# Early products handed to GpSimd, one first load to ScalarE, single last tiles: a dynamic-convolution kernel with a new order

## The chip, the cores and the metric

One core of a Trainium2 chip runs the whole kernel. The metric is the device time of one execution in microseconds (us); every time below is from the chip. The core has five engines with queues of their own: TensorE (PE; its weight loads are PEld), VectorE (DVE), ScalarE (ACT), GpSimd (POOL) and SyncE (SP, which here only issues transfers). Each executes its instructions in the order in which they were written, and waits at an instruction until what it depends on is done.

## The reference

```python
w = exp(weight_gen - max(weight_gen, -1));  w = w / (sum(w, -1) + 1e-9)      # [8, 4224, 8 heads, 7 taps]
out[b, s, h, :] = sum over k of w[b, s, h, k] * x_padded[b, s + k, h, :]     # causal, 6 zeros ahead; 24 columns a head
xn = (out - mean(out)) / sqrt(var(out) + 1e-6) * g_ln                        # over the 192 columns
result = out + relu(xn @ w_ch1) @ w_ch2                                      # 192 -> 768 -> 192
```

x is [8, 4224, 192] in float32; `w_ch1` and `w_ch2` arrive as float64, and the kernel rebuilds their float32 values from the words.

## The kernel before

The 33,792 tokens are cut into 128 runs of 264 consecutive tokens, one run on each partition (16 partitions for each of the 8 batches), so a "token" below is one of 264 columns of 128 tokens. Three pipelines run side by side.

*Softmax* (`softmax`), in pieces of 4, 8 and then 12 tokens: maximum on VectorE (`max`), subtraction on GpSimd (`sub`), exponential on ScalarE (`exp`), sum on VectorE (`sum`; for two pieces on TensorE), logarithm on ScalarE (`log`), and a second subtraction on GpSimd (`less`). A last exponential on ScalarE (`expw`) writes one chunk's weights to PSUM.

*Convolution* (`conv`), in chunks: two of 2 tokens, then chunks of 4, later of 6. They start at tokens 0, 2, 4, 8, 12, 16, ..., so the first is S0, the second S2, the third S4, the fourth S8, the fifth S12. A chunk has four products of x with weights: `c0` (taps 1, 2), `c1` (taps 3, 4), `c2` (tap 0) and `c3` (taps 5, 6). The three with two taps write `pr` buffers, of which there are five. VectorE makes them, but in the first `PMUL` = 3 chunks GpSimd makes `c3`, from a copy of the weights in SBUF that one more exponential (`keep`) leaves there. The first three chunks are summed over the taps by TensorE (`z0` to `z3`) and copied out by ScalarE (`copy`). From the fourth on, two transfers add pairs of products (`d0`, `d1`) and four GpSimd additions (`a0` to `a3`) finish the sum `y`.

*Norm and feed-forward* (`norm` and what follows): mean and variance of each token come from ScalarE (`sums`, `squares`, one activation with an accumulator for each token); where the part's start lies below `STATS` = 8 (the first two parts, tokens 0 to 7) from VectorE (`stats`). Then `rstd` on ScalarE, `newton` on VectorE, the scaled tokens `xh` on ScalarE. Groups of 4 tokens are split into two halves of float16 (`hi` on ScalarE, `lo` on GpSimd) and transposed by a transfer (`turn`, line 762); the first two groups are transposed by TensorE (`tp`, `thi`, `tlo`). A group has three units of first-layer products (`unit`, line 780) with two PSUM buffers to write to; each is emptied by a ScalarE ReLU (`relu`) and then a VectorE operation that writes the low half (`hlo`, line 798). After a group's second unit come the two halves of the second layer of the group before it (`p0`, `p1`, line 832), and VectorE adds the result to `y` (`f`, line 884), which is stored (`u`). The last group has no unit behind it: its four tiles are made one by one (`output`, line 853), two in one PSUM bank, and `merge` adds each pair by one VectorE operation of 384 columns and stores it.

The weights of both layers are loaded, rebuilt and split in the first 55 us (`load_weights`, `from_double`, `w_scale`, `weights`), on the same engines.

The order is written out by hand: `PLACE` gives each operation its position, by name and count, and `Plan.order` sorts by it and hands out buffers. An engine's order is the order of its operations in `PLACE`. The costs passed to `op` take no part in it here.

Of the kernel before, what the change touches and what calls it, by code (L numbers as in the profile page):

```python
# [26 lines left out]
PMUL = 3  # L27
STATS = 8
# [11 lines left out]
    'wload': (0, 1, 15, 26, 98, 102, 176, 495, 321, 482, 657, 761, 837, 1034, 613, 1145, 1282, 1182, 951, 1438,  # L40
        1515, 1614, 1730,),
    'load': (2, 3, 5, 7, 9, 22, 43, 95, 105, 145, 143, 174, 92, 244, 288, 208, 297, 414, 325, 484, 497, 660,
        569, 626, 644, 719, 851, 815, 920, 942, 918, 1001, 1066, 1240, 1236, 1303, 1205, 1365, 1353, 1467, 1476,
        1619, 1541, 1592, 1669, 1749, 1853, 1832, 1814, 1980, 2003, 1949,),
    'w_load': (45, 13, 20,),
    'w_gain': (40, 38, 29,),
    'w_load2': (32,),
    'w_as': (88,),
    'w_ap': (90,),
    'w_av': (96, 99,),  # L50
    'w_an': (107,),
    'w_cs': (53,),
    'w_cp': (52,),
    'w_cv': (58, 60,),
    'w_cn': (80,),
    'w_s1': (113, 118,),
    'w_d': (150, 124,),
    'w_h': (127, 123,),
    'w_l': (155, 126,),
    'w_lc': (166, 130,),  # L60
    'w_m': (169, 172, 135, 133,),
    'w_c2s': (73, 103, 120,),
    'w_c2p': (71, 94, 125,),
    'w_c2v': (76, 79, 108, 110, 134, 138,),
    'w_c2n': (83, 116, 142,),
    'w_s2': (148, 156, 185,),
    'w_d2': (178,),
    'w_h2': (175, 164, 183,),
    'w_l2': (184, 181, 189,),
    'w_lc2': (200, 202, 194,),  # L70
    'max': (4, 11, 54, 64, 188, 281, 355, 559, 594, 537, 769, 881, 907, 1073, 1096, 1211, 1320, 1225, 1430,
        1502, 1679, 1770, 1960,),
    'sub': (6, 16, 59, 81, 193, 378, 448, 565, 599, 679, 779, 887, 972, 1091, 1124, 1261, 1400, 1415, 1513,
        1598, 1759, 1811, 2007,),
    'exp': (8, 21, 63, 111, 215, 382, 467, 592, 637, 709, 795, 903, 1023, 1105, 1148, 1276, 1412, 1459, 1581,
        1645, 1822, 1849, 2023,),
    'sum': (10, 25, 234, 390, 492, 601, 645, 721, 834, 946, 1032, 1138, 1178, 1279, 1435, 1511, 1605, 1676,
        1835, 1860, 2034,),
    'log': (12, 28, 86, 152, 249, 409, 498, 604, 658, 765, 858, 969, 1036, 1160, 1251, 1341, 1458, 1524, 1608,
        1699, 1856, 1869, 2060,),  # L80
    'less': (14, 31, 87, 160, 276, 421, 510, 606, 691, 771, 883, 987, 1058, 1193, 1257, 1344, 1478, 1559, 1650,
        1742, 1859, 1937, 2093,),
    'expw': (17, 30, 35, 56, 97, 139, 151, 199, 235, 266, 327, 356, 329, 434, 473, 516, 540, 623, 656, 703, 722,
        783, 820, 910, 960, 996, 1017, 1080, 1111, 1210, 1203, 1280, 1359, 1372, 1402, 1503, 1494, 1594, 1564,
        1678, 1721, 1775, 1796, 1888, 1944, 1972, 2058, 2145, 2102, 2104,),
    'keep': (18, 39, 65,),
# [16 lines left out]
    'copy': (50, 69, 119,),  # L103
    'stats': (61, 74, 144, 141,),
    'rstd': (77, 147, 209, 279, 354, 426, 502, 585, 693, 802, 895, 1002, 1102, 1201, 1307, 1420, 1501, 1623,
        1713, 1817, 1926, 2018, 2119, 2214, 2280, 2338,),
    'newton': (91, 153, 219, 285, 359, 432, 507, 591, 696, 804, 901, 1003, 1106, 1204, 1309, 1433, 1510, 1627,
# [10 lines left out]
    'thi': (136, 180,),  # L118
    'tlo': (159, 186,),
# [19 lines left out]
    'sums': (131, 168, 191, 187, 222, 242, 268, 258, 323, 310, 338, 334, 380, 399, 413, 411, 478, 457, 486, 490,  # L139
# [149 lines left out]
def kernel(  # L289
# [309 lines left out]
    def norm(pa):  # L599
# [3 lines left out]
        def row(i):  # L603
            if S0 < STATS:
                i = {1: 3, 2: 4}[i]
            return at(s4)[:, i, :n]
# [538 lines left out]
```

## Time and profile before

| | before |
|---|---|
| runs (us) | 843.34, 845.62, 844.35: median 844.35 |
| profiled execution (us) | 843.82, its span 842.0, mean granted clock 0.994 |
| TensorE busy | 821.4 us, 98% of the span |
| VectorE, GpSimd, ScalarE busy | 736.5 (87%), 701.6 (83%), 683.8 us (81%) |
| first TensorE instruction, first unit, last product's end | 8.4, 52.7, 837.5 us |
| data moved | 140.88 MB, 167 GB/s over the span |

Instructions are named by the line of the kernel that made them. A row of a timeline gives the start, the time and how many like instructions were put together, and in square brackets how long the engine had stood idle before and what ended that. TensorE's granted clock is 1.00 at 2.4 GHz and 0.50 at 1.2 GHz.

### The profile page before, as it was taken

How to read it: one execution, taken by the hardware profiler on the slowest of the kernel's cores; microseconds unless marked ns; L12 is line 12 of the kernel's file. 1: busy time of each engine (PE TensorE's matmuls, PEld its weight loads, DVE VectorE, ACT ScalarE, POOL GpSimd, SP SyncE). 2: the span in 40 equal slices, each digit the busy share in tenths (PEclk: the TensorE clock that was granted, in tenths of full speed). 3: DMA queues.
4: the chain of work that ended last, by engine and by line, in shares of the span. 5: the costliest groups of instructions: out<-in, count | busy, mean ns of one | idle time of the engine just before them, and what ended most of it. 6: DMA issues, size and time to landing. Idle time of an engine off the chain costs nothing.

```text
span 842.0 us, 37407 instructions
## 1 busy us (share of the span) xinstructions
PE 821.4 (98%) x16724; PEld 811.3 (96%) x16724; DVE 736.5 (87%) x685; ACT 683.8 (81%) x1774; POOL 701.6 (83%) x402
## 2 busy tenths in 40 slices
PE   6889999999999999999999999999999999999997
PEld 5669999999999999999999999999999999999997
DVE  7999999999999999999999999999989896745332
ACT  3899998898998899898888979988888878776431
POOL 4999999999999999999999999899798879624000
PEclk9889999999999999999999999999999999999999
DMA  9997997989999997889878997777877766352432
GB/s 228 206 211 153 221 162 170 204 160 205 193 195 191 199 215 167 178 186 215 190 153 202 188 217 174 164 185 163 180 153 162 165 145 129 78 116 68 80 65 58
DMA packets 133887, 140.88 MB, mean 167 GB/s; under 512 B 104294, under 2 KB 106222, under 8 KB 133726
## 3 DMA queue, kind: packets, MB, share of 16 engines
q1 hardware_dynamic: 120190, 88.16, 45.9%
q0 software_dynamic: 13536, 50.34, 30.8%
q8 instruction: 130, 2.13, 1.0%
q14 instruction: 31, 0.25, 0.1%
HBM read 36.43 MB, written 25.95 MB: 74 GB/s over the span
## 4 chain that ended last, share of the span: by engine, by line
PE 82%; DVE 11%; issue 2%; POOL 2%; ACT 1%; DMA 1%; SPq 1%; DVEq 0%; POOLq 0%; ACTq 0%
PE po L832 41%; PE ph L780 40%; DVE pr L535 6%; DVE hlo L798 2%; DVE y L535 1%; POOL y L538 1%; DMA x<-in_x_dram 1%; PE ph L861 1%; DVE y L884 1%; POOL pr L541 1%; ACT hh L796 0%; DVE mx L466 0%; ACT junk L611 0%; DVE sm L482 0%; DVE s L628 0%
## 5 line engine op out<-in xcount | busy, mean ns | idle before, releaser
L538 POOL TENSOR_TENSOR y<-y,pr 128x1152 f32<-128x1152 f32 (+1 forms) x188 | 488.3, 2625 | 13.0 <-DVE y L535 4.3
L780 PE MATMUL ph<-xT,c_w 64*128 64x256 f16 x7128 | 412.9, 269 | 1.9 <-DVE hlo L798 1.3
L780 PEld LDWEIGHTS <-c_w 64*128 64x128 f16 x7128 | 386.2, 94 | 3.1 <-issue 2.9
L832 PE MATMUL po<-c_w2h,hh 64*128 64x192 f16 x3120 | 388.0, 243 | 1.1 <-DVE y L884 1.1
L832 PE MATMUL po<-c_w2l,hh 64*128 64x192 f16 x3120 | 388.0, 243 | 0.0
L832 PE MATMUL po<-c_w2h,hlo 64*128 64x192 f16 x3120 | 388.0, 243 | 0.0
L535 DVE TENSOR_TENSOR pr<-x,wn 128x2304 f32<-128x2304 f32 (+2 forms) x147 | 333.2, 2276 | 4.3 <-POOL y L538 2.5
L832 PEld LDWEIGHTS <-hh 64*128 64x128 f16 x6240 | 309.7, 94 | 1.4 <-issue 1.3
L798 DVE SCALAR_TENSOR_TENSOR hlo<-ph,hh 128x1024 f16<-128x1024 f32 x198 | 239.4, 1217 | 73.1 <-ACT hh L796 72.6
L796 ACT ACTIVATE hh<-ph 128x1024 f16<-128x1024 f32 x198 | 200.2, 1014 | 84.8 <-PE ph L780 80.6
L832 PEld LDWEIGHTS <-hlo 64*128 64x128 f16 x3120 | 177.6, 94 | 0.0
L758 POOL TENSOR_TENSOR hl<-xh,hl 128x768 f16<-128x768 f32 x64 | 114.7, 1828 | 49.1 <-ACT hl L756 48.3
L686 ACT ACTIVATE xh<-y,s 128x192 f32<-128x192 f32 x264 | 125.8, 536 | 17.2 <-DVE s L674 12.1
L616 ACT ACTIVATE junk<-y,s 128x192 f32<-128x192 f32 x256 | 115.8, 452 | 7.9 <-PE po L832 1.8
L541 POOL DMA_DIRECT2D pr<-pr x94 | 93.2, 1054 | 26.6 <-DVE pr L535 22.1
L611 ACT ACTIVATE junk<-y 128x192 f32<-128x192 f32 x256 | 92.1, 360 | 12.5 <-PE po L832 4.1
L884 DVE SCALAR_TENSOR_TENSOR y<-po,c_fs,y 128x768 f32<-128x768 f32 (+1 forms) x83 | 67.9, 835 | 7.4 <-PE po L832 7.2
L535 DVE TENSOR_TENSOR y<-x,wn 128x1152 f32<-128x1152 f32 (+2 forms) x50 | 59.9, 1199 | 0.0
L756 ACT ACTIVATE hl<-xh 128x768 f16<-128x768 f32 x64 | 53.4, 836 | 1.6 <-PE po L832 0.7
L611 ACT ACTIVATION_READ_ACCUMULATOR junk<-y 128x1 f32 x256 | 48.1, 188 | 0.0
L616 ACT ACTIVATION_READ_ACCUMULATOR junk<-y,s 128x1 f32 x256 | 47.9, 187 | 0.0
L486 POOL TENSOR_TENSOR e<-e,sm 128x672 f32<-128x672 f32 (+2 forms) x23 | 37.8, 1645 | 6.6 <-ACT sm L484 6.6
(86 smaller groups left out, 308.3 us busy)
## 6 DMA issues: line engine op xcount, KB each, us to landing
pr<-pr POOLq DMA_DIRECT2D x68, 576.0 KB, 6.1
x<-in_x_dram SPq DMA_DIRECT2D x34, 576.0 KB, 6.0
out_dram<-y SPq DMA_DIRECT2D x34, 576.0 KB, 4.9
pr<-pr POOLq DMA_DIRECT2D x26, 384.0 KB, 5.0
w<-in_weight_gen_dram SPq DMA_DIRECT2D x21, 336.0 KB, 5.1
x<-in_x_dram SPq DMA_DIRECT2D x14, 384.0 KB, 6.2
out_dram<-y SPq DMA_DIRECT2D x13, 384.0 KB, 5.2
x<-in_moe_w_ch_dram SPq DMA_DIRECT2D x1, 1152.0 KB, 11.3
```

The costliest lines, as they stand in the source:

```text
L535: E.tensor_tensor(out=ov, in0=xv, in1=wv, op=ALU.mult)
L538: Q.tensor_tensor(out=flat(0), in0=flat(0), in1=flat(k), op=ALU.add)
L541: return Q.dma_start(flat(to), flat(k), accum_op=ALU.add, max_dma_last_dim=CHUNK * D * 4)
L611: A.activation(junk, at(y)[:, j, :], AF.Identity, scale=-SQ / D, accum_out=at(s4)[:, 3, t : t + 1])
L616: A.activation(junk, at(y)[:, j, :], AF.Square, scale=SQ, bias=at(s4)[:, 3, t : t + 1], accum_out=at(s4)[:, 0, t : t + 1])
L686: A.activation(paired(xh, t), at(y)[:, i, :].rearrange("p (c q) -> p c q", q=P // 2), AF.Identity, bias=row(2 if quick else 3)[:, g + t : ...
L758: lambda xh=xh, hl=hl: Q.tensor_tensor(out=halves(hl, True), in0=pairs(xh), in1=halves(hl, False), op=ALU.subtract),
L780: T_.matmul(ph[:, r, v * 2 * P : (v + 1) * 2 * P], W["w1"][rows, WB[r][c], w, f : f + P], xv[rows, a, c, :, :], start=(v == 0 and k == 0), ...
L796: lambda: A.activation(at(hh)[:, us, :], at(ph), AF.Relu), [ph], [(hh, u)])
L798: lambda: V.scalar_tensor_tensor(out=at(hlo)[:, us, :], in0=at(ph), scalar=0.0, in1=at(hh)[:, us, :], op0=ALU.max, op1=ALU.subtract),
L832: made.append(T_.matmul(at(po)[:, z, e * D : (e + 1) * D], token(b, 2 * z + e, j)[rows], W[w][rows, j, :], start=(ph == 0 and e == 0 and k ...
L884: V.scalar_tensor_tensor(out=ysl, in0=at(po)[:, zs[0] : zs[-1] + 1, : 2 * D], scalar=W["fs"][:, 0:1], in1=ysl, op0=ALU.mult, op1=ALU.add)
```

## The change

Five things are edited, and `PLACE` is replaced as a whole (2400 positions before, 2408 after).

- The second of the two first loads of x is issued on ScalarE's queue. ScalarE's table load and its `minus` activation become planned operations; by the new positions they stand ahead of that load (`table` 1, `minus` 4, load 5).
- `PMUL` is 4, so GpSimd makes `c3` of the fourth chunk too; `PTWO` has it make `c1` of the second chunk.
- `STATS` is the tuple `(4,)`: the first part's statistics (tokens 0 to 3) are now ScalarE's.
- `last` replaces `output` for the last four tiles: each has a PSUM bank and a VectorE operation of 192 columns of its own. The first two are stored together, the other two one by one.
- The first exponential waits for `table`, the matmuls with `minus` for `minus`.

```diff
-PMUL = 3
-STATS = 8
+PMUL = 4
+STATS = (4,)
+PTWO = (2,)
...
-    A.preload_act_table_set("natural_log_exp_and_others")
...
-    A.activation(minus, ident, AF.Copy, scale=-1.0)
...
-            def first(o, m):
+            def first(o, m, E=SY):
                 src = bass.AP(tensor=xf.tensor, offset=(C - PAD + o) * D,
                               ap=[[C * D, PB - 1], [PB * C * D, B], [1, m * D]])
-                SY.dma_start(X[B:P, o : o + m, :].rearrange("p t d -> p (t d)"), src)
+                E.dma_start(X[B:P, o : o + m, :].rearrange("p t d -> p (t d)"), src)
...
-            sp(want, lambda: first(cut, PAD + n - cut), [], [("x", "h"), *cols], dma_ns((PAD + n - cut) * D * 4), "load")
+            op("ACT", 620, want, lambda: first(cut, PAD + n - cut, A), w=[("x", "h"), *cols],
+               dma=dma_ns((PAD + n - cut) * D * 4), kind="load")
+            op("ACT", 1300, ("table", 0), lambda: A.preload_act_table_set("natural_log_exp_and_others"), w=["table"])
+            op("ACT", 310, ("minus", 0), lambda: A.activation(minus, ident, AF.Copy, scale=-1.0), ["table"], ["minus"])
...
-            if c < PMUL and i == 3:
+            if c < PMUL and (i == 3 or i == 1 and t0 in PTWO):
                 op("Pool", q_ns(2 * nd), (f"c{i}", t0), lambda k=k: mul(k, 2, Q), [*xr, (e, "w", c)], w)
...
-        quick = S0 < STATS
+        quick = S0 in STATS
...
+    def last(gp, t, s):
+        e = t % 2
+        if e == 0:
+            gp["po"] = Buf("ph")
+        po, ks = gp["po"], triples(gp)
+
+        def mm():
+            for k, (b, j, w) in enumerate(ks):
+                T_.matmul(at(po)[:, e, :D], token(b, t, j), W[w][:, j, :], start=k == 0, stop=k == len(ks) - 1)
+
+        op("PE", 1490, ("o", s), mm, whole(gp), [(po, e), "pe"], lat=360.0)
+        y, j = ycol(gp["pa"], gp["g"] + t)
+
+        def final():
+            V.scalar_tensor_tensor(out=at(y)[:, j, :], in0=at(po)[:, e, :D], scalar=W["fs"][:, 0:1],
+                                   in1=at(y)[:, j, :], op0=ALU.mult, op1=ALU.add)
+
+        op("V", v_ns(D, 63), ("f", s), final, [(po, e), "fs"], [(y, j)])
+        if t > 0:
+            i, n = (j, 1) if t > 1 else (j - 1, 2)
+            t0 = chunks[-1]["S"] + i
+            sp(("u", s), lambda: SY.dma_start(tokens(out, t0, n), at(y)[:, i : i + n, :].rearrange("p t d -> p (t d)")),
+               [(y, i + q) for q in range(n)], [], dma_ns(n * D * 2))
...
     for t in range(NT):
-        output(prev, t, C)
+        last(prev, t, C)
```

The order that the old and the new `PLACE` give each engine at the start (operation and token at which its chunk, softmax piece or part starts; `w_...` are weight operations, and numbers count them):

```
SyncE before    w S0, w S4, x first a, x first b, x first f, x S2, x S4, w_load 1, w S12, w_load 2, x S8, w S24, gain, load2, gain, gain, x S12, w_load 0
SyncE after     w S0, x first a, w S4, x first f, x S2, w S12, x S4, w_load 1, w_load 2, x S8, load2, w_load 0, gain, gain, w S24, gain, x S12
VectorE before  max S0, sum S0, max S4, c0 S0, c2 S0, sum S4, c1 S0, c0 S2, c1 S2, c2 S2, c2 S4, c1 S4, c0 S4, max S12, w_cv 2x, stats S0, max S24, c1 S8, c0 S8, stats S2, w_c2v 2x, c2 S8, c3 S8, newton S0, w_av 2x, c2 S12, w_c2v 2x, c0 S12
VectorE after   max S0, sum S0, c0 S0, c2 S0, max S4, c1 S0, sum S4, c0 S2, c2 S2, max S12, c0 S4, c2 S4, w_cv 2x, c0 S8, c2 S8, c1 S8, w_c2v 2x, c1 S4, newton S0, w_c2v, max S24, w_av, w_c2v, w_av, c0 S12, c2 S12
GpSimd before   sub S0, less S0, sub S4, less S4, c3 S0, c3 S2, sub S12, c3 S4, d0 d1 S8, sub S24, less S12, a0 a1 a2 a3 S8, d0 a0 d1 a1 a2 S12, d0 S16, less S24, a3 S12
GpSimd after    sub S0, less S0, sub S4, c3 S0, less S4, c1 S2, c3 S2, sub S12, c3 S8, d0 a0 a1 S8, c3 S4, less S12, d1 S8, sub S24, d0 S12, a2 S8, d1 S12, a3 S8, a0 a1 a2 S12, d0 S16, a3 S12, less S24
```

TensorE's order of operations is the same in both. From about token 96 on the other engines' orders are the same again, but for the end.

## Rows read from the trace of the kernel before

**Rows 1.** Chain of waits in time order, from 800 us: start, us, what.
```profile
802.86 1.96 PE ph L780 x36
804.83 2.97 PE po L832 x72
...
831.47 6.06 PE ph L861 x72
```

**Rows 2.** Timeline of TensorE, first units: start, us, instruction, [idle before].
```profile
57.23 2.14 PE L780 MATMUL ph<-xT,c_w 64*128 64x256 f16 x36 [0.32 <-DVE hlo L798]
...
71.86 4.11 PE L780 MATMUL ph<-xT,c_w 64*128 64x256 f16 x72
```

**Rows 3.** Windows: window, length, busy PE PEld DVE ACT POOL, clock, DMA share, GB/s.
```profile
30.00:40.00 10.00, 6.95 (x34) 4.98 (x33) 9.53 (x16) 9.02 (x22) 9.37 (x7) 0.82 0.87 216
40.00:50.00 10.00, 8.26 (x32) 6.12 (x32) 9.69 (x17) 9.23 (x28) 9.92 (x8) 0.67 1.00 210
```

**Rows 4.** Timeline of VectorE, up to 31 us.
```profile
5.11 0.61 DVE L466 TENSOR_REDUCE mx<-w 128x64 f32<-128x448 f32 x1
7.30 0.95 DVE L535 TENSOR_TENSOR pr<-x,wn 128x768 f32<-128x768 f32 x1 [1.58 <-DMA x<-in_x_dram]
...
13.08 3.41 DVE L535 TENSOR_TENSOR pr<-x,wn 128x1536 f32<-128x1536 f32 x2
...
29.70 0.95 DVE L535 TENSOR_TENSOR y<-x,wn 128x768 f32<-128x768 f32 x1
```

**Rows 5.** Timeline of GpSimd, up to 40 us.
```profile
9.77 0.97 POOL L486 TENSOR_TENSOR e<-e,sm 128x448 f32<-128x448 f32 x1 [2.58 <-ACT sm L484]
...
15.44 1.55 POOL L535 TENSOR_TENSOR pr<-x,e 128x768 f32<-128x768 f32 x1 [3.20 <-PE ph L560]
...
19.91 2.90 POOL L535 TENSOR_TENSOR pr<-x,e 128x1536 f32<-128x1536 f32 x1 [1.15 <-ACT e L502]
...
25.81 2.00 POOL L486 TENSOR_TENSOR e<-e,sm 128x672 f32<-128x672 f32 x1
27.14 8.14 POOL L538 TENSOR_TENSOR y<-y,pr 128x768 f32<-128x768 f32 x4
35.22 0.87 POOL L541 DMA_DIRECT2D pr<-pr  x1
```

**Rows 6.** Instruction groups of VectorE by shape: count, busy us, mean ns, idle before.
```profile
L535 DVE TENSOR_TENSOR pr<-x,wn 128x1536 f32<-128x1536 f32 x41 | 70.9, 1744 | 0.1
...
L628 DVE BATCH_NORM_STATS2 s<-y 128x6 f32<-128x384 f32 x4 | 2.2, 560 | 0.0
...
L955 DVE SCALAR_TENSOR_TENSOR po<-pr,po 128x384 int32<-128x384 int32 x3 | 1.7, 552 | 0.0
L884 DVE SCALAR_TENSOR_TENSOR y<-ph,c_fs,y 128x384 f32<-128x384 f32 x2 | 1.2, 618 | 4.4 <-PE ph L861 4.4
```

**Rows 7.** Timeline of SyncE: transfers as they are issued.
```profile
2.11 1.93 SPq L428 DMA_DIRECT2D x<-in_x_dram  x2
...
66.05 1.54 SPq L762 DMA_TRANSPOSE xT<-hl  x1
```

**Rows 8.** Timeline of ScalarE, up to 50 us.
```profile
6.30 0.27 ACT L498 ACTIVATE wn<-e 128x112 f32<-128x112 f32 x1 [0.75 <-POOL e L486]
...
15.24 0.48 ACT L573 COPY y<-ph 128x384 f32<-128x384 f32 x1 [3.89 <-PE ph L560]
...
46.23 0.36 ACT L611 ACTIVATE junk<-y 128x192 f32<-128x192 f32 x1
...
48.23 0.60 ACT L1071 ACTIVATE c_w2h<-hlo,c_r 128x384 f16<-128x384 f32 x1
```

**Rows 9.** Transfers of the whole run by line: count, KB, median us to landing.
```profile
xT<-hl SPq DMA_TRANSPOSE x64, 3.9
```

**Rows 10.** Transfers issued after 830 us: count, KB each, median us to landing.
```profile
out_dram<-y SPq DMA_DIRECT2D x1, 384.0 KB, 3.3
out_dram<-y SPq DMA_DIRECT2D x2, 192.0 KB, 2.5
```

More of the change, by code (lines that the diff above doesn't have):

```diff
@@ L39 @@
 PLACE = {
[L40 to L85, printed above, removed]
@@ L86 @@
-    'keep': (18, 39, 65,),
[16 rows of a table removed]
[L103 to L107, printed above, removed]
[10 rows of a table removed]
-    'thi': (136, 180,),
-    'tlo': (159, 186,),
[19 rows of a table removed]
-    'sums': (131, 168, 191, 187, 222, 242, 268, 258, 323, 310, 338, 334, 380, 399, 413, 411, 478, 457, 486, 490,
[6 rows of a table removed]
@@ L146 @@
-    'squares': (154, 173, 195, 206, 259, 247, 275, 277, 332, 346, 341, 349, 388, 401, 419, 422, 481, 468, 499,
[15 rows of a table removed]
-    'turn': (239, 282, 308, 317, 400, 410, 471, 477, 549, 554, 618, 639, 652, 727, 755, 740, 825, 848, 862, 939,
[3 rows of a table removed]
-    'halo': (316, 563, 768, 1130, 1345, 1638, 2061,),
-    'unit': (197, 203, 212, 220, 227, 243, 260, 267, 284, 302, 309, 326, 344, 351, 367, 384, 391, 406, 423, 430,
[10 rows of a table removed]
-    'relu': (204, 214, 217, 231, 236, 251, 270, 283, 296, 313, 319, 340, 358, 373, 377, 393, 404, 418, 431, 442,
[10 rows of a table removed]
@@ L189 @@
-    'hlo': (207, 216, 223, 237, 253, 261, 278, 287, 305, 318, 324, 343, 362, 379, 383, 402, 412, 420, 436, 451,
[14 rows of a table removed]
-    'hop': (246, 286, 331, 368, 407, 446, 485, 522, 555, 588, 628, 665, 699, 735, 772, 809, 844, 878, 915, 948,
[16 rows of a table removed]
+    'wload': (0, 3, 10, 47, 62, 142, 182, 479, 278, 544, 664, 766, 842, 1039, 623, 1150, 1287, 1187, 956, 1443,
+        1520, 1619, 1735,),
+    'load': (2, 5, 6, 8, 13, 21, 52, 78, 88, 148, 178, 151, 245, 318, 186, 289, 339, 425, 410, 482, 627, 666,
+        565, 629, 651, 724, 856, 820, 925, 946, 923, 1006, 1072, 1245, 1240, 1308, 1210, 1369, 1358, 1472, 1481,
+        1624, 1546, 1597, 1674, 1754, 1858, 1837, 1819, 1985, 2008, 1954,),
@@ new lines @@
+    'table': (1,),
+    'minus': (4,),
+    'w_load': (28, 15, 18,),
+    'w_gain': (31, 51, 41,),
+    'w_load2': (24,),
+    'w_as': (96,),
+    'w_ap': (98,),
+    'w_av': (102, 108,),
+    'w_an': (112,),
+    'w_cs': (57,),
+    'w_cp': (58,),
+    'w_cv': (61, 66,),
+    'w_cn': (101,),
+    'w_s1': (116, 119,),
+    'w_d': (135, 124,),
+    'w_h': (154, 125,),
+    'w_l': (157, 127,),
+    'w_lc': (170, 132,),
+    'w_m': (175, 174, 140, 137,),
+    'w_c2s': (79, 91, 138,),
+    'w_c2p': (80, 92, 126,),
@@ new lines @@
+    'w_c2v': (83, 85, 97, 105, 141, 145,),
+    'w_c2n': (89, 113, 147,),
+    'w_s2': (150, 167, 204,),
+    'w_d2': (181,),
+    'w_h2': (184, 176, 180,),
+    'w_l2': (189, 185, 196,),
+    'w_lc2': (195, 190, 202,),
+    'max': (7, 25, 42, 100, 194, 230, 308, 585, 574, 625, 774, 886, 912, 1079, 1101, 1216, 1325, 1230, 1435,
+        1507, 1684, 1775, 1965,),
+    'sub': (9, 26, 56, 110, 201, 345, 426, 596, 577, 685, 784, 892, 975, 1095, 1129, 1266, 1405, 1420, 1518,
+        1603, 1764, 1816, 2012,),
@@ new lines @@
+    'exp': (11, 30, 70, 122, 217, 373, 439, 603, 643, 714, 800, 908, 1028, 1110, 1153, 1281, 1417, 1464, 1586,
+        1650, 1828, 1854, 2028,),
+    'sum': (12, 34, 259, 402, 448, 606, 648, 726, 839, 951, 1037, 1143, 1183, 1284, 1440, 1516, 1610, 1681,
+        1840, 1865, 2039,),
+    'log': (14, 37, 95, 161, 275, 422, 481, 613, 662, 770, 863, 974, 1041, 1165, 1256, 1347, 1463, 1529, 1613,
+        1704, 1861, 1874, 2065,),
+    'less': (16, 38, 103, 172, 282, 430, 484, 616, 697, 775, 887, 990, 1063, 1198, 1261, 1349, 1483, 1564, 1655,
+        1746, 1864, 1941, 2097,),
@@ new lines @@
+    'expw': (17, 32, 44, 45, 107, 149, 162, 209, 225, 251, 303, 354, 372, 446, 438, 523, 537, 631, 661, 708,
+        727, 788, 825, 916, 965, 1001, 1022, 1085, 1117, 1215, 1208, 1285, 1364, 1377, 1407, 1508, 1499, 1599,
+        1569, 1683, 1726, 1781, 1801, 1893, 1949, 1977, 2063, 2150, 2107, 2109,),
+    'keep': (19, 35, 60, 46,),
[16 rows of a table added]
+    'copy': (55, 73, 118,),
+    'sums': (63, 75, 155, 144, 192, 203, 243, 248, 257, 281, 325, 335, 348, 341, 397, 389, 409, 423, 470, 468,
[7 rows of a table added]
+    'squares': (67, 81, 166, 173, 197, 211, 260, 286, 267, 292, 327, 351, 360, 344, 416, 392, 412, 427, 475,
[7 rows of a table added]
@@ new lines @@
+    'rstd': (86, 139, 219, 294, 365, 431, 509, 592, 698, 807, 900, 1007, 1108, 1206, 1312, 1425, 1506, 1628,
+        1718, 1822, 1931, 2023, 2124, 2219, 2285, 2343,),
+    'newton': (93, 153, 223, 298, 367, 437, 514, 597, 701, 809, 906, 1008, 1111, 1209, 1314, 1438, 1515, 1632,
[10 rows of a table added]
+    'thi': (129, 187,),
+    'tlo': (146, 193,),
+    'stats': (131, 128,),
[27 rows of a table added]
+    'turn': (242, 284, 324, 334, 404, 420, 474, 464, 539, 551, 619, 646, 660, 732, 760, 745, 830, 853, 867, 943,
[3 rows of a table added]
+    'halo': (276, 614, 773, 1135, 1350, 1643, 2066,),
@@ L221 @@
+    'unit': (200, 207, 215, 224, 231, 246, 264, 270, 288, 304, 312, 329, 347, 353, 371, 386, 393, 411, 428, 434,
[10 rows of a table added]
+    'relu': (208, 216, 221, 234, 241, 255, 272, 283, 297, 315, 332, 338, 356, 366, 383, 399, 406, 421, 436, 447,
[10 rows of a table added]
+    'hlo': (210, 218, 226, 240, 256, 266, 280, 295, 301, 321, 343, 346, 363, 379, 385, 405, 414, 424, 445, 450,
[14 rows of a table added]
+    'hop': (249, 291, 331, 375, 415, 453, 487, 522, 559, 591, 633, 667, 704, 740, 777, 815, 849, 883, 920, 953,
[16 rows of a table added]
 }
@@ L468, in softmax @@
              lambda: Q.tensor_tensor(out=at(e)[:, :m], in0=a3(wb), in1=wide(mx), op=ALU.subtract), [wb, mx], [e])
-        step("ACT", a_ns(m * K), "exp", lambda: A.activation(a3(wb), at(e)[:, :m], AF.Exp), [e], [wb])
+        step("ACT", a_ns(m * K), "exp", lambda: A.activation(a3(wb), at(e)[:, :m], AF.Exp), [e, "table"], [wb])
         if S0 in PESUM:
@@ L603, in row @@
         def row(i):
-            if S0 < STATS:
+            if S0 in STATS:
                 i = {1: 3, 2: 4}[i]
@@ L1030, in mm @@
                     T_.matmul(at(z)[:, b, :h], minus, hi()[:, q], start=False, stop=True)
-            op("PE", 2.2 * n, ("w_l", 0), mm, [(dg, i), *r], [z], lat=400.0)
+            op("PE", 2.2 * n, ("w_l", 0), mm, [(dg, i), "minus", *r], [z], lat=400.0)
             op("ACT", a_ns(n, 150), ("w_lc", 0),
@@ L1076, in mm @@
                 T_.matmul(at(z)[:, h % 2, :tn], minus, w2f[:, o : o + tn], start=False, stop=True)
-            op("PE", 2.2 * tn, ("w_l2", 0), mm, [dq, (w2r, h), ("w2h", h)], [(z, h % 2)], lat=400.0)
+            op("PE", 2.2 * tn, ("w_l2", 0), mm, [dq, "minus", (w2r, h), ("w2h", h)], [(z, h % 2)], lat=400.0)
             op("ACT", a_ns(tn, 150), ("w_lc2", 0),
```

239 rows, old and new, of the table PLACE are left out of this document.

## The prediction

> **What bounds the kernel now.** I read the chain of waits first, at its late end. From 800 us on it is TensorE alone: units of first-layer products of 1.96 us (36 matmuls), halves of second-layer products of 2.97 us (72), the last four tiles in 6.06 us up to 837.53, then one VectorE operation and its store [rows 1]. Then the timeline of TensorE: the third unit starts at 57.23 us, and what it waited for is `hlo`, the VectorE operation that empties the first unit's PSUM buffer [rows 2]. From there to 837.53 are 780.3 us; the 196 units and 130 halves that are left and the last tiles are 196 x 1.96 + 130 x 2.97 + 6.06 = 776.3 us. So only 4.0 us are lost after that point. The middle is TensorE's own work, and its order of operations is the same in both kernels. What can change is the time at which that third unit starts, those 4.0 us, and the 4.5 us behind the last product (842.0 - 837.5).
>
> What sets the start is read from windows before it: between 30 and 50 us VectorE is busy 9.53 and 9.69 of 10 us, GpSimd 9.37 and 9.92, ScalarE 9.02 and 9.23, while TensorE has gaps and its granted clock has fallen [rows 3]. VectorE is full from its first product at 7.30 us on, which had waited for a load of x [rows 4]. GpSimd gets full later: before 25 us it waited 2.58, 3.20 and 1.15 us in front of three instructions [rows 5]. So I forecast by a ledger of VectorE up to the first `hlo`, and check it against GpSimd and ScalarE.
>
> **The ledger of VectorE.** Removed: an early product of the second chunk (128x768, 0.95 us), the k=5,6 product of the fourth chunk (128x1536, 1.744), two statistics (0.56 each) [rows 4, 6]. Neighbours overlap by 0.08 (two of 128x1536 take 3.41 us, 1.744 + 1.66), so net 0.87 + 1.66 + 2 x 0.48 = 3.5 us. It is worth that if nothing else comes late, and 0 if another engine sets the start.
>
> The loads: on SyncE the two first loads of x took 1.93 us of issue [rows 7], 0.97 each. ScalarE takes one; the other moves ahead of the second load of weights. The exponential that the first product needs ends at 6.57 (6.30 + 0.27 [rows 8]); the product began at 7.30. So 0.7 us at most are won, and 0 if the transfers themselves are the limit. I take 0.7, since what it waits for is issued about one weight load sooner. On ScalarE the issue stands between the table load and the softmax's first exponential, in idle time: 0, or 1.0 (SyncE's issue time) if that exponential comes late.
>
> The Trainium skill limits this: "DMA: Bandwidth & Descriptors", section "Issuing engines are not separate DMA queues", has it that loads started on several engines run on the same 16 DMA engines, and only time of issue is saved. By that rule bytes ahead of the load still count, and with a term of 0 the sum would be 0.7 smaller; no row before the change tells which.
>
> What it costs: the second load of weights comes about 1 us later, and the maximum over it (0.61 us [rows 4]) moves from idle time before 7.30 to behind two products: -0.5. The sum over it then waits for a GpSimd subtraction (0.97, the row of its shape [rows 5]) and a ScalarE exponential (0.27 at a quarter of its size [rows 8], so 0.3 to 1.1, I take 0.6), under the cover of one product (0.87): -0.7 (0 to -1.2).
>
> GpSimd: it gets a 128x768 product (1.55 us) and a 128x1536 one (2.90) [rows 5], 4.45 us together. Its new order, laid out by those rows: the subtraction of the second softmax ends at about 9.5 (two VectorE products and the maximum behind 6.6, then 0.97); the first chunk's product 11.05; the second softmax's other subtraction 12.0; two products of the second chunk 15.1; a subtraction of the third softmax (1.33, from 25.81 to 27.14) 16.4; the new 128x1536 product 19.3; a transfer issued (0.87) and two additions (2.03 each, four in 8.14) 24.3; the third chunk's product 27.2; the third softmax's other subtraction 28.5. Before, that one ended at 27.14: 3.1 of the 4.45 us go into the idle time above. By a ScalarE exponential (0.27 to 0.54, I take 0.3) it releases the first VectorE product of the fifth chunk, at 28.8. Before, VectorE came to that chunk at 29.70 [rows 4]; with the terms above (0.7 - 0.5 - 0.7 + 3.5 = 3.0) it comes at 26.7, or at 27.8 since two weight operations of 0.55 [rows 6] are put ahead of the chunk. It waits 1.0: -1.0 (0 to -3.0).
>
> A page speaks against giving products to GpSimd at all: the Trainium skill, "GPSIMD Engine Reference", section "3.1 Elementwise — side-by-side cycle accounting", has 4497 against 2293 ns for one two-input operation, a ratio of 1.96. Here it is 2.90 against 1.744, 1.66, measured in this kernel. By the page's ratio the two 128x1536 products would take 0.5 us longer each, and the gain would be 1.0 us smaller; I go by the rows.
>
> ScalarE: four sums and four squares come to it for the first four tokens. Two and two take 2.00 us (46.23 to 48.23 [rows 8]), so 4.0. It stood idle for 3.89 us at 15.24 [rows 8], about where they now stand, and for 0.98 + 0.77 between 30 and 50 [rows 3]. I cost them at 0; with no cover they delay the weight copies ahead of the first unit by 4.0, which is part of rival 2.
>
> Ledger: 3.0 - 1.0 = 2.0 us earlier at the first `hlo`, and the third unit with it; 0 and 4.2 are the ends.
>
> **Behind the start.** The transpose of the third group was issued at 66.05 [rows 7] and lands 3.9 later [rows 9], at 70.0; its unit starts at 71.86 [rows 2]. TensorE will want it 2.0 earlier with 1.9 of slack, and VectorE delivers its part about 2 us earlier. GpSimd doesn't: it is 1.4 late at 28 us, less a subtraction of 1.33 that the new order puts behind the fifth chunk's additions. I leave the 4.0 us lost there as they are (bounds: 1 saved to 2.5 added).
>
> **The end.** The last operation takes 192 columns instead of 384. A column costs (1.744 - 0.95) / 768 = 1.03 ns, so 0.2 of its 0.618 us go [rows 6]. The third tile's operation lies under the last tile's matmuls. The last store is 96 KB instead of 192: between 384 and 192 KB the landing fell from 3.3 to 2.5 us [rows 10]; 0.4 more if that goes on, 0 if what is left is fixed; I take 0.2. The matmuls are the same 72 with other banks: 0. End: 0.4 (0.2 to 0.6).
>
> **Sum.** 2.0 + 0.4 = 2.4 us. The profiled execution took 843.8 us (span 842.0); less 2.4 that is 841.4. The median of the runs, 844.35, lies 0.5 above it; less 2.4 it is 841.9, my forecast.
>
> **Rivals.**
> 1. The cover holds everywhere: 3.5 of VectorE's work in full, 0.7 of the loads, 0.4 of the end, and some 0.5 of the 4.0 lost later: 5.1, so 839.3. For it: the idle time of GpSimd in [rows 5] is 6.9 us against 4.45 added. Against: that time lies behind waits for other engines. Chance 0.20.
> 2. GpSimd or ScalarE sets the start: GpSimd is 9.92 of 10 us busy from 40 us on [rows 3], and ScalarE's 4.0 us may find only part of its idle time. The start gains 0 to 1 and the end its 0.4: 843.0 to 844.0. Chance 0.25.
> 3. Slower, by TensorE's clock. The gaps let the granted clock fall, to means of 0.82 and 0.67 in two windows [rows 3]; the lower level, 1.2 of 2.4 GHz, is 0.5, so it held for (0.18 + 0.33) x 10 / 0.5 = 10 us. It was over before the units began. With other gaps ahead of the second-layer weights the fall can come later and reach into the first units, which then lose half of that time for good: 5 us if all of it lies there. 841.9 + 5 = 846.9, or 848.9 if the start isn't earlier either. It decides at a granted clock of 0.5 under the first units; up to 2.4 us lost it only eats the gain. Chance 0.12.
>
> **How the numbers follow.** The forecast has the remaining 0.43, and a range of its own of 840.5 to 843.3. 0.3% (2.5 us) is about what a measurement can tell from no change. Faster by more is below 841.8: rival 1 and nearly half of the forecast's case (0.2), with a little of rival 2 by the spread of the runs, 0.44 in all. Slower by more is above 846.9: the upper half of rival 3 and a bad run, 0.09. The rest is 0.47. The range 839.2 to 845.2 leaves out the better half of rival 1 and most of rival 3.
>
> **What would show it.** VectorE's first product at 6.6; a wait of VectorE at 27 to 29 us for the fifth chunk's exponential; the third unit at 55.2; the last VectorE operation at 0.42 us, and 4.1 us from the last product to the end of the span. A third unit not before 57, a granted clock below 1.00 under the units, or new waits of TensorE between 65 and 110 us would prove it wrong.

## The result

The changed kernel is slower: 851.94 us (median of 6 runs, 851.65 to 852.53) against 844.39 for the kernel before (6 runs, 843.12 to 845.62). The ratio is 1.0092 with a 95% interval of 1.0079 to 1.0105, +7.5 us where 2.4 less was forecast. In the profiled executions the spans are 850.8 and 842.0 us, 8.8 apart.

**Profile after.** I read ScalarE's timeline first, since [rows 8] put the exponential ahead of the first product at 6.30. ScalarE in the changed kernel (start, length, instruction, idle before it and its releaser; ACTq is its issue of transfers), and then the first exponential in the kernel before:

```profile
0.74 1.28 ACT L437 ACT_TABLE_LOAD   x1 [0.74 <-PEq L1158]
2.33 0.31 ACT L438 ACTIVATE minus<-ident 128x128 f16<-128x128 f32 x1 [0.31 <-POOL ident L377]
7.02 1.49 ACTq L430 DMA_DIRECT2D x<-in_x_dram  x1
8.62 0.39 ACT L474 ACTIVATE w<-e 128x224 f32<-128x224 f32 x1 [5.98 <-issue]
...
10.53 0.27 ACT L503 ACTIVATE wn<-e 128x112 f32<-128x112 f32 x1 [0.75 <-POOL e L491]
```

```profile
4.38 0.39 ACT L469 ACTIVATE w<-e 128x224 f32<-128x224 f32 x1 [1.75 <-POOL e L468]
```

ScalarE is free at 2.64 and does nothing until it issues its load at 7.02. The softmax's first exponential comes behind that, at 8.62; the kernel before had it at 4.38. "<-issue" means that the profile shows nothing that ScalarE waited for. The compiled program does. In its list of ScalarE's instructions the load carries a wait:

```
2 L438 ACTIVATE minus<-ident 128x128 [waits Pool_49]
3 L430 DMA x<-in_x_dram 120x1x768 [waits DMAHW2_49]
4 L474 ACTIVATE w_64<-e_96 128x224 [waits DMAHW0_49,Pool_49]
```

DMAHW0 to DMAHW7 are eight completion counters, which the compiler gives in turn to the transfers that SyncE and ScalarE issue (GpSimd's have counters of their own). In SyncE's list of the same program the ninth and tenth transfer wait for DMAHW0 and DMAHW1, the next for DMAHW3. ScalarE's load, the fourth transfer by its place in the written order, has thus been counted as the eleventh; how the compiler comes to count it there is not shown, but with one ScalarE instruction fewer ahead of it, it is counted third (experiment 2). It gets the third transfer's counter and may not be issued before that one has landed. The third is the second softmax's weights. The chain of waits of the changed kernel shows the handover (start, length, what):

```profile
2.56 4.44 DMA w<-in_weight_gen_dram
7.02 9.44 DMA x<-in_x_dram
```

The weights land at 7.00, the load is issued at 7.02 and lands at 16.46. VectorE has both delays, in answer to [rows 4]:

```profile
9.04 0.39 DVE L487 TENSOR_REDUCE sm<-w 128x32 f32<-128x224 f32 x1 [5.36 <-ACT w L474]
10.83 0.95 DVE L540 TENSOR_TENSOR pr<-x,wn 128x768 f32<-128x768 f32 x1 [1.41 <-ACT wn L503]
...
16.48 0.95 DVE L540 TENSOR_TENSOR pr<-x,wn 128x768 f32<-128x768 f32 x1 [3.71 <-DMA x<-in_x_dram]
```

The first product is 3.5 us late (10.83 against 7.30). The product at 16.48 is the first chunk's second one of two taps (`c1` S0); it is the first to read what ScalarE's load brings, and waits 3.7 more for it. TensorE, in answer to [rows 2], and its waits from 50 to 300 us (what waited, for what: us in total, times, longest):

```profile
59.69 4.11 PE L785 MATMUL ph<-xT,c_w 64*128 64x256 f16 x72 [0.74 <-ACT c_w2l L1109]
64.20 2.14 PE L785 MATMUL ph<-xT,c_w 64*128 64x256 f16 x36 [0.41 <-DVE hlo L803]
```

```profile
PE po L837 <- issue: 1.4, 2, 1.1
PE ph L785 <- DVE hlo L803: 1.3, 3, 0.7
PE ph L785 <- DMA xT<-hl: 1.2, 1, 1.2
```

The third unit starts at 64.20 instead of 57.23: 7.0 of the 8.8 us. From there to the end of the last product (846.24) it is 782.0 instead of 780.3, 1.7 more, 1.2 of it a wait for a transposed tile that the kernel before did not have. From the last product to the end of the span it is 4.6 instead of 4.5. The granted clock fell again ahead of the units, and was back under them, where 72 matmuls take 4.11 us as in [rows 2] (window, length, busy PE PEld DVE ACT POOL, clock, DMA share, GB/s; compare [rows 3]):

```profile
40.00:50.00 10.00, 8.95 (x34) 6.23 (x33) 9.79 (x14) 8.95 (x29) 8.78 (x6) 0.73 0.84 201
50.00:60.00 10.00, 6.94 (x29) 4.47 (x29) 9.90 (x14) 7.67 (x24) 10.00 (x9) 0.76 0.86 210
60.00:70.00 10.00, 8.94 (x162) 8.53 (x159) 7.87 (x12) 9.64 (x26) 9.32 (x7) 1.00 0.76 146
```

### The profile page after: what moved, and what is told of

It is laid out like the page before. It is cut to its first block, busy times and chain, and to the rows that moved or that the text cites. A ratio compares the mean times of both kernels' runs of the same rounds, so it can differ in the third digit from the quotient of the medians.

```text
span 850.8 us, 37434 instructions
## 1 busy us (share of the span) xinstructions
PE 824.3 (97%) x16724; PEld 810.8 (95%) x16724; DVE 733.5 (86%) x683; ACT 687.7 (81%) x1791; POOL 705.7 (83%) x404
## 4 chain that ended last, share of the span: by engine, by line
PE 85%; POOL 4%; ACT 4%; DVE 3%; issue 2%; DMA 2%; SPq 0%; DVEq 0%; POOLq 0%
PE po L837 42%; PE ph L785 41%; POOL y L543 2%; DVE pr L540 2%; DMA x<-in_x_dram 1%; PE ph L565 1%; ACT junk L621 1%; DVE hlo L803 1%; POOL pr L546 1%; POOL hl L763 1%; PE ph L866 1%; ACT junk L616 1%; DMA w<-in_weight_gen_dram 1%; ACT hh L801 0%; PE ph L1104 0%
## 5 line engine op out<-in xcount | busy, mean ns | idle before, releaser
L621 ACT ACTIVATE junk<-y,s 128x192 f32<-128x192 f32 x260 | 117.6, 452 | 9.9 <-PE po L837 3.7
L491 POOL TENSOR_TENSOR e<-e,sm 128x672 f32<-128x672 f32 (+2 forms) x23 | 35.6, 1548 | 8.5 <-ACT sm L489 8.5
```

The lines of the kernel that those rows point to most:

```text
L621: A.activation(junk, at(y)[:, j, :], AF.Square, scale=SQ, bias=at(s4)[:, 3, t : t + 1], accum_out=at(s4)[:, 0, t : t + 1])
```

## Experiments

"The start" below is the start of the third unit (before 57.23, after 64.20). A time that follows "against" is that of the kernel before, run again beside the experiment; the ratio is taken to it, with its 95% interval in brackets.

**1. The load back on SyncE, all else as changed.**
```
-  op("ACT", 620, want, lambda: first(cut, PAD + n - cut, A), ...
+  op("SP", 620, want, lambda: first(cut, PAD + n - cut, SY), ...
```


> The changed kernel with one edit: the second first load of x goes back to SyncE, in the same position. Counter theory (ScalarE's load waits until the transfer of the second weights has landed, since the two are given the same completion counter, and ScalarE holds the softmax behind it): 841 to 844 us, the first exponential back at 4.4 us. Queue theory (a transfer is slow to start and to land on ScalarE's own queue): the same 841 to 844. Handover theory (GpSimd's and ScalarE's added work and the new order cost the time): stays at 850 or above.

844.62 us against 843.92, ratio 1.0006 [0.9997, 1.0016]: the whole loss is gone, and no gain is left. This kernel shows the rest of the change without the accident. VectorE:

```profile
6.58 0.95 DVE L540 TENSOR_TENSOR pr<-x,wn 128x768 f32<-128x768 f32 x1 [1.41 <-ACT wn L503]
...
29.09 1.75 DVE L540 TENSOR_TENSOR pr<-x,wn 128x1536 f32<-128x1536 f32 x1 [0.64 <-ACT wn L503]
...
52.06 1.74 DVE L540 TENSOR_TENSOR pr<-x,wn 128x1536 f32<-128x1536 f32 x1
55.11 1.22 DVE L803 SCALAR_TENSOR_TENSOR hlo<-ph,hh 128x1024 f16<-128x1024 f32 x1 [1.30 <-ACT hh L801]
```

The first product is at 6.58 (forecast 6.6), the fifth chunk at 29.09 behind a wait of 0.64 (28.8, 1.0). VectorE is free for the first `hlo` at 53.8; in the kernel before it came to that `hlo` at 55.96, without a pause. So the ledger's 2.0 us are there, as 2.2. But `hlo` waits 1.30 for ScalarE's ReLU of the first unit, and the start is 56.39, 0.84 earlier. The first unit itself starts at 51.88, behind the last weight products (TensorE; then windows as above):

```profile
47.42 0.91 PE L1104 MATMUL ph<-hlo,xh 128*128 128x384 f32 x2 [2.00 <-ACT xh L1095]
...
51.17 0.52 PE L1105 MATMUL ph<-c_w2h,minus 128*128 128x384 f16 x1
51.88 4.11 PE L785 MATMUL ph<-xT,c_w 64*128 64x256 f16 x72 [0.18 <-ACT c_w2l L1109]
```

```profile
46.00:48.00 2.00, 0.58 (x2) 0.40 (x3) 2.00 (x3) 2.00 (x6) 2.00 (x2) 1.00 0.99 243
48.00:50.00 2.00, 2.00 (x7) 0.95 (x5) 2.00 (x3) 0.57 (x1) 2.00 (x3) 0.59 0.87 265
50.00:52.00 2.00, 1.81 (x7) 0.59 (x7) 2.00 (x3) 1.84 (x7) 2.00 (x3) 0.56 1.03 270
```

The same in the kernel before:

```profile
49.18 0.91 PE L1075 MATMUL ph<-hlo,xh 128*128 128x384 f32 x2 [1.74 <-ACT xh L1066]
...
51.82 0.33 PE L1076 MATMUL ph<-c_w2h,minus 128*128 128x384 f16 x1
52.72 4.19 PE L780 MATMUL ph<-xT,c_w 64*128 64x256 f16 x72 [0.58 <-ACT c_w2l L1080]
```

```profile
48.00:50.00 2.00, 0.82 (x3) 0.46 (x4) 2.00 (x3) 2.00 (x6) 2.00 (x3) 1.00 0.95 197
50.00:52.00 2.00, 1.99 (x8) 0.78 (x6) 2.00 (x5) 1.91 (x9) 2.00 (x3) 1.00 1.02 300
```

TensorE idles for 2.00 us, from 48 us on the granted clock is 0.59 and 0.56, for the most part its lower level, and the weight products take 4.3 us (47.42 to 51.69) instead of the 3.0 (49.18 to 52.15) that they took before at 1.00. They are 1.3 us longer, as much as the start misses the ledger by; experiment 9 tests how much of it is the clock's.

**2. ScalarE's load one place sooner, ahead of the `minus` activation.**
```
-    'load': (2, 5, 6, 8, 13, ...
+    'load': (2, 3.5, 6, 8, 13, ...
```


> The changed kernel with ScalarE's load of x one place earlier, between the table load and the activation that makes minus; there it is given a counter that no transfer holds, and has no wait. Counter theory: issue at 2.0 to 3.0 us, exponential at 4.4, 841 to 844 us. Queue theory: issue late or landing over 8 us all the same, 848 us or more. Handover theory: 850 or more.

844.84, 1.0007 [0.9997, 1.0016]. One engine, one transfer, the same bytes; only its place, and with it its counter, differs. It is now among the first eight transfers, and SyncE's eighth, the ninth of all, is the first that carries a wait:

```profile
0.77 1.47 ACTq L430 DMA_DIRECT2D x<-in_x_dram  x1
2.33 0.31 ACT L438 ACTIVATE minus<-ident 128x128 f16<-128x128 f32 x1 [0.30 <-POOL ident L377]
4.40 0.39 ACT L474 ACTIVATE w<-e 128x224 f32<-128x224 f32 x1 [1.76 <-POOL e L473]
```

Issuing a load from ScalarE is therefore not what costs. Nor does it win anything: the first product is at 7.10, behind a wait of 1.89 for x, later than with both loads on SyncE (6.58): the two now run at once, and the one needed first lands 5.5 us after its issue, where the median of the two was 5.0 in experiment 1. This agrees with "DMA: Bandwidth & Descriptors" of the Trainium skill, section "Issuing engines are not separate DMA queues": only issue time is saved. In the trace the start is 57.98, 1.6 later than in experiment 1; the times of the two (844.84 and 844.62) do not tell them apart.

**3. The kernel before, with this one load on ScalarE.** The edit is the `op("ACT", 620, ...)` of the change, alone.

> The kernel before with this one edit alone: the second first load of x on ScalarE, behind table load and minus. It is given the counter of the first load of x (landing at 7.3 us). Counter theory: issue at about 7.3, exponential at about 8.8 instead of 4.4, product of taps 3 and 4 not before 15; 848 to 853 us. Queue theory: slower too, 846 to 853, with the issue at 2.7. Handover theory: 844, no change.

852.26, 1.0097 [1.0080, 1.0114]: this edit alone costs as much as the whole change. The load's counter is that of another third transfer, the first load of x, which lands at 6.99; ScalarE's issue comes at 7.01, the exponential at 8.61, the start at 66.28.

**4. The counter of a small transfer.** The 12 KB load goes to the third place.
```
-    'load': (2, 5, 6, 8, 13, ...
+    'load': (2, 5, 2.5, 8, 13, ...
```


> The changed kernel with two SyncE loads exchanged: the 12 KB load of x goes ahead of the second weights, so it is the third transfer, and ScalarE's load is given its counter. Counter theory: ScalarE's load is issued when that small transfer has landed, at 4.6 to 5 us instead of 7.0, the exponential at 6.1 to 6.6 instead of 8.6, and 845.5 to 849 us. Queue theory: no change, 851 to 853.

851.28, 1.0075 [1.0058, 1.0092]. ScalarE's issue follows the new holder of the counter, 6.03 instead of 7.02, and the exponential comes at 7.74, the start at 60.81. The direction is the theory's, the size smaller than I expected: the 12 KB, issued at 2.56 behind two larger transfers, land only at 6.01. In the traces the start is 3.4 us earlier than in the changed kernel and the span 2.3 shorter (848.5 against 850.8), so 1.2 of it is lost again behind the start; at which point is not shown. By the medians it is 0.7, and the intervals of the two ratios overlap: how much of the time is won back is not sharp.

**5. ScalarE held without the load.** Experiment 1 with a small activation of ScalarE that reads the second softmax's weights, put where the load stood. Its result is unused.
```
+    'hold': (5.5,),
...
+            if q["S"] == 4:
+                op("ACT", 310, ("hold", 0), lambda wb=q["w"]: A.activation(
+                    plan.pools["junk"][0][:, 0:8], at(wb)[:, 0, 0:8], AF.Copy), [q["w"]], [])
```


> The kernel of e1 (load back on SyncE) with a small ScalarE activation at the load's old place that reads the second softmax's weights, and so holds ScalarE until they have landed; the load itself isn't late. If holding the softmax is the price: the first exponential at about 7.3 instead of 4.4, the third unit 2 to 3 us later than in e1 (56.4), 846.5 to 848 us. If the price lies in the late landing of x, nothing: 844 to 845.

847.97, 1.0037 [1.0021, 1.0053]. ScalarE is held up to 7.18, the exponential is at 7.29, the start at 60.84, 4.5 after experiment 1's; in the changed kernel it was 7.8 after. So holding ScalarE is 4.5 of the 7.8, and the issue's 1.5 us behind it together with the late landing are the other 3.3. Some of the 4.5 is the clock's: the granted clock is 0.50 from 50 to 56 us and 0.81 from 56 to 58, and the 72 matmuls of the first two units take 4.48 instead of 4.11. In time, by the ratios, it is 2.6 of 7.3 us, with intervals of about 1.5 each: both parts are there, their shares are not sharp.

**6. The changed end alone.** The kernel before with the function `last`.
```
-        output(prev, t, C)
+        last(prev, t, C)
```


> The kernel before with the new end alone: four tiles with a PSUM bank and a VectorE operation each, stores of two, one and one token. Prediction: 0.2 from the last operation and 0.2 from the last store, 0.4 us faster (0 to 0.6); the end behind the last product 4.1 us instead of 4.5. A rival: the third tile's store holds SyncE and delays the last one, 0.2 to 0.5 us slower.

844.35, 1.0004 [0.9995, 1.0013]. VectorE's and then SyncE's last rows:

```profile
835.17 0.74 DVE L867 SCALAR_TENSOR_TENSOR y<-ph,c_fs,y 128x192 f32<-128x192 f32 x2 [2.14 <-PE ph L861]
838.06 0.74 DVE L867 SCALAR_TENSOR_TENSOR y<-ph,c_fs,y 128x192 f32<-128x192 f32 x2 [2.15 <-PE ph L861]
```

```profile
838.51 1.18 SPq L874 DMA_DIRECT2D out_dram<-y  x2
```

The two operations of a pair run back to back behind the second tile: 0.74 for both, where one took 0.62 [rows 6]. Each tile has a PSUM bank of its own, but the two banks are one buffer, and in the compiled program the first operation waits for the products of both tiles, which stand ahead of it in the written order. The third tile's store is then issued right ahead of the last one: 1.18 of issue instead of 0.54. The 96 KB land in 2.1 us instead of 2.5 [rows 10]. Behind the last product it is 4.46 us, as before.

**7. The final operations apart.** Each, with its store, is placed ahead of the next tile's products, in the kernel before with `last`, and in experiment 1's kernel (with places of its own).
```
-    'f': (..., 2393.5, 2395, 2397.2, 2398,),
+    'f': (..., 2392.5, 2393.5, 2394.5, 2398,),
```


> Before with the changed end alone, and each tile's final operation and store placed ahead of the next tile's products in the program's order. Theory A (the final operations of a pair ran together at 838.06 in the version without this, because both were issued behind the second tile's products and so waited for them): they run apart, the first about 1.5 us ahead of the second; the last store is issued behind one of 0.42 us alone; end of the program 4.1 us after the last product instead of 4.46, time 0.2 to 0.5 below before. Theory B (the two halves of the bank are released together, or the store's own issue sets the end): again a pair of 0.74, end 4.4 to 4.5, time within 0.2 of before.

> The changed kernel with the load back on SyncE, and each of the last final operations and stores ahead of the next tile's products. Theory A: end 4.1 us after the last product instead of 4.5, time 0.2 to 0.5 below the one without (844.62), 0.0 to 0.4 below before with the start's 0.4 us of the last product. Theory B: end 4.4 to 4.5, 844.4 to 844.8.

845.05, 1.0007 [0.9998, 1.0015], and 846.05, 1.0017 [1.0008, 1.0027]. The pair does come apart and the end shrinks to 3.9 us (843.3 - 839.4), more than theory A asked. But TensorE pays for it; its rows in the first of the two:

```profile
834.11 0.24 PE L861 MATMUL ph<-c_w2h,hh 128*128 128x192 f16 x1 [0.59 <-DVE y L867]
...
837.75 0.24 PE L861 MATMUL ph<-c_w2h,hh 128*128 128x192 f16 x1 [0.51 <-DVE y L867]
```

The next tile waits for VectorE's read: 1.1 us lost (0.59 and 0.51), 0.6 won. It writes the other bank of the buffer (`ph` is [128, 2, 512] in float32, and `last` takes one of its two banks for each tile of a pair), so the two touch different banks; in the compiled program the wait goes by the buffer. A buffer of its own for each of the two tiles, which would need no such wait, was not tried.

**8. The statistics of the first part back on VectorE** (experiment 1 with `STATS = (0, 4)`).

> The kernel of e1 with the first part's statistics back on VectorE (about 4.0 us less on ScalarE, 1.0 more on VectorE). If ScalarE takes back what VectorE wins: the first unit up to 1.5 us earlier than in e1 (51.9), 843.0 to 844.2 us. If VectorE is the bound: 845 to 846. If TensorE's low clock ahead of the units is: no change, 844.6.

844.70, 1.0005 [0.9994, 1.0016], start at 56.35 against 56.39. ScalarE's four added sums and squares are covered; they are not what lies ahead of the first unit.

**9. TensorE kept busy in its gap.** Experiment 1 with ten products of the identity with itself, written to a buffer from which nobody reads them, where TensorE idled for 2.00 us.
```
+    'busy': (169,),
...
+    for k in range(10): T_.matmul(at(zb)[:, k % 2, :P], ident, ident, start=True, stop=True)
```


> The kernel of e1 with ten products of the identity with itself (2.1 us at the upper clock, results unused) in TensorE's gap of 45.4 to 47.4 us, ahead of the second layer's weight products. If the fall of the granted clock at 48.8 us, which stretches these products from 3.0 to 4.3 us, takes the gain: clock 1.00 from 46 to 54 us, the first unit at 50.4 to 50.8 instead of 51.9, 843.0 to 843.6 us. If ScalarE's copies set the first unit: no change, 844.6.

845.17, 1.0009 [0.9999, 1.0019]. Windows, then TensorE's timeline, then its waits from 50 to 300 us:

```profile
46.00:48.00 2.00, 2.00 (x17) 1.82 (x16) 2.00 (x3) 2.00 (x6) 2.00 (x2) 1.00 1.01 249
48.00:50.00 2.00, 1.64 (x7) 0.75 (x5) 2.00 (x3) 1.23 (x3) 2.00 (x3) 1.00 0.95 246
50.00:52.00 2.00, 1.65 (x20) 1.07 (x20) 2.00 (x3) 1.94 (x10) 2.00 (x3) 1.00 0.98 250
```

```profile
49.69 0.91 PE L1112 MATMUL ph<-hlo,xh 128*128 128x384 f32 x2 [0.36 <-DVE xT L728]
...
51.12 4.11 PE L786 MATMUL ph<-xT,c_w 64*128 64x256 f16 x72 [0.35 <-ACT c_w2l L1117]
55.63 2.14 PE L786 MATMUL ph<-xT,c_w 64*128 64x256 f16 x36 [0.41 <-DVE hlo L804]
...
96.06 4.10 PE L786 MATMUL ph<-xT,c_w 64*128 64x256 f16 x72 [1.74 <-DMA xT<-hl]
```

```profile
PE ph L786 <- DMA xT<-hl: 1.7, 1, 1.7
PE ph L786 <- DVE hlo L804: 1.7, 3, 0.9
PE po L838 <- issue: 1.3, 1, 1.3
```

The clock stays at 1.00, and the start is 55.63: 1.6 earlier than before, and 0.8 earlier than in experiment 1. So of the 1.3 us that experiment 1 missed, the clock is 0.8; behind it the third pair of weight products waits 0.36 for VectorE, and the first unit 0.35 for ScalarE. What is won is all given back: at 96 us TensorE waits 1.74 for a transposed tile, and the last product ends at 838.2, against 837.5 before.

**10. GpSimd relieved.** Experiment 9 with `PMUL = 3`, and with `PTWO = ()`: one early product goes back to VectorE in each, of 2.9 us on GpSimd in the first (1.75 on VectorE) and of 1.54 in the second (0.95 on VectorE; the 1.7 us that was expected there is too much).

> The changed kernel with the load back on SyncE and the ten unused products in the gap, and GpSimd without its fourth early product (it goes back to VectorE, as before). Theory A (the gain at the start is lost because GpSimd's stretch from 50 to 110 us is full, so that its subtraction ahead of a transpose comes late): GpSimd runs up to 2.9 us earlier there, TensorE's wait for a transposed tile goes from 1.7 to under 0.7, last product 836.9 to 837.5, time 0.7 to 1.3 below the one with four (845.17). Theory B (VectorE's stretch is as full, and the 1.7 us that it takes on come back as waits for the first unit's input): first unit or third unit 0.5 to 1.5 later than 51.12 and 55.63, time within 0.4 of 845.17 or above.

> The same with GpSimd's fourth product kept, and its second product of the chunk at tile 2 back on VectorE instead. Theory A as in the one with three products: wait for a transposed tile under 0.7, time 0.7 to 1.3 below 845.17. Theory B: VectorE's second chunk is 1.7 us longer at 13 to 30 us, all of VectorE's queue behind it moves by up to 1.7, third unit 56.4 to 57.3, time within 0.4 of 845.17 or above.

847.16, 1.0033 [1.0022, 1.0044], and 845.21, 1.0011 [1.0002, 1.0020]. The starts are 56.07 and 56.17, 0.4 and 0.5 later than in experiment 9, and the wait for a transposed tile is still 1.4 and 1.6 us. The trace of the first is of its shortest execution, 845.28, so what makes the others 2 us longer is not shown. Theory A falls: GpSimd's subtraction ahead of the transposes came at 87.96 with three products, 87.57 with four. It had waited for VectorE just before, and VectorE then waits for it (GpSimd's row, then VectorE's, with three products):

```profile
83.19 0.88 POOL L547 DMA_DIRECT2D pr<-pr  x1 [0.84 <-DVE hlo L804]
```

```profile
97.29 1.75 DVE L541 TENSOR_TENSOR pr<-x,wn 128x1536 f32<-128x1536 f32 x1 [1.24 <-POOL y L544]
```

Between 50 and 110 us the two engines hand work to each other with hardly any slack, so handing work from GpSimd back to VectorE does not bring the transposed tile forward. Which of them would have to lose how much stays open. No version beat the kernel before.

## Why the prediction was wrong

**The step that failed** is on ScalarE's load: "On ScalarE the issue stands between the table load and the softmax's first exponential, in idle time: 0, or 1.0 (SyncE's issue time) if that exponential comes late." ScalarE's time there was idle, but the issue could not use it: the load waits for the holder of its completion counter. The exponential is 4.24 us late, the product that needs the load about 8 (16.48 against 8.52 in experiment 1). Experiments 1, 2 and 3 show the cause from three sides: the load off ScalarE, the load on ScalarE without a wait, and the load alone on ScalarE; in experiment 4 the issue moves with the transfer that holds the counter. The prediction's bound of 1.0 counted what an issue takes and left out what it waits for. The kernel before has such waits on SyncE's own list, from its ninth transfer on; I did not read that list.

**The rival on the slow side** named TensorE's clock under the first units. That did not happen in the changed kernel: the 72 matmuls of the first two units take 4.11 us there. The fall is ahead of them, and it only ate gain. It does reach into them in experiment 5, for 0.4 us.

**The ledger** was right where the load does not disturb it (experiment 1): 6.58 for 6.6, 29.09 for 28.8, a wait of 0.64 for 1.0, VectorE free 2.2 us earlier for 2.0. "The third unit with it" was wrong: the start gained 0.84. Next late was not VectorE but the weight products, 1.3 us longer at the lower clock. Where the clock stays at 1.00, the start gains 1.6 of VectorE's 2.2 us (experiment 9). The size in experiment 1 is that of rival 2, a start 0 to 1 us earlier, but not by ScalarE's added work: without it the start does not move (experiment 8). For GpSimd's it is not shown, since what GpSimd gave up went to VectorE (experiment 10).

**ScalarE's statistics at 0** held (experiment 8).

**Behind the start**, "I leave the 4.0 us lost there as they are" held in experiment 1 (780.8 from the start to the last product, 780.3 before), and failed once the start came earlier still (782.6 in experiment 9), within the bound of 2.5 that it gave.

**The end** was forecast at 0.4 and came to nothing, though both its terms are there: the store gained 0.4 where 0.2 was taken, one operation takes 0.42 instead of 0.62. "The third tile's operation lies under the last tile's matmuls" is the part that failed: it runs behind them, since it waits for the products of both tiles of the buffer, and its store's issue of about 0.6 stands ahead of the last store (experiment 6). With each operation put ahead of the next tile's matmuls, these stop for 1.1 us in all (experiment 7).

## What to carry to other kernels

A transfer that is moved to another engine can get a wait there for an earlier transfer, and all of that engine's queue stands behind it: look which transfer holds its completion counter and when that one lands. Placed ahead of one activation, the same load cost nothing that the times tell (844.84 against 844.62 us). And where several engines are full at the start, time won on one is worth what the next late thing allows; here that was weight products at the lower clock behind a gap of 2 us, and after them a transposed tile. An operation on one bank of a two-bank buffer can wait for the other bank's work too.

## Not expected of the hardware

ScalarE takes 1.47 to 1.60 us to issue a load that SyncE issues in 0.89 to 1.03. In the changed kernel one load of 360 KB landed 9.4 us after an issue at 7.02, beside the large weight loads, and the other of the same size 4.9 after one at 1.48. With ten unused products in the gap of 2.00 us the granted clock stayed at 1.00 where it had been 0.59 and 0.56.
